# 2:4-sparse linear layer on one core: a first weight piece cut in two, a new hand-written order of the front, and unpacking DMAs in another order

## The chip, the core and the metric

One core of a Trainium2 chip. Five engines run their own instruction streams and meet at semaphores: TensorE (PE, matmuls; its weight loads are shown apart as PEld), VectorE (DVE), ScalarE (ACT), GpSimd (POOL) and SyncE (SP, which here issues DMAs). Sixteen DMA engines move the data. The metric is the device time of one execution in microseconds; smaller is better. Before the change it is 235.28 us, the median of 3 runs (235.22 to 235.59).

## The reference

```python
B, S, D = 16, 512, 1024            # x: (16, 512, 1024), w: (1024, 1024), b: (1024), all bf16
wg = w.reshape(D // 4, 4, D)       # groups of 4 along k
mag = jnp.abs(wg)
order = jnp.argsort(mag, 1)
thr = jnp.take_along_axis(mag, order[:, 2:3, :], 1)
mask = mag >= thr                  # the two largest of each four stay
wp = (wg * mask).reshape(D, D)
out = einsum("bsd,df->bsf", x, wp) + b
```

So the weight matrix is pruned 2:4 along k, and 8192 tokens are multiplied with it: 64 tiles of 128 tokens, each with k = 1024 and 1024 output columns.

## The kernel before

**Two stretches.** The main loop (lines 286 to 303) is plain: each tile of 128 tokens takes 16 matmuls of 512 columns (8 blocks of k by two halves of the output), DVE adds the bias out of PSUM, ACT issues the store. It needs x transposed (done by transposing DMAs, `issue_batch`) and the pruned weights in natural order of k, `wp_nat[h]` (h is the half of the output columns). Ahead of it stands the front, which has to load, prune and unpack the weights while PE already works on the first T = 10 tiles.

**How the weights come.** `w` is seen as `(g p m) f`: g is a half of k (512 rows), p the partition, m the place in a group of four. So a group's four values lie in one partition, and pruning is elementwise work on DVE. It goes by *pieces* `(g, c0, c1)`: half of k and a range of output columns. For each piece `abs_piece` (A) makes magnitudes, on DVE or on ACT, and `prep_piece` (P) runs seven DVE operations (lines 131 to 141): max and min of pairs, the threshold, the mask, the product back into `w_gh`.

**How PE uses them.** For the first half of k (g = 0), the token tiles are transposed on PE itself with an identity (`transpose_half`, T) in the order of (p, m), and copied out of PSUM by ACT (`copy_half`, C), so that the pruned weights can be used in the layout they have. For the second half (g = 1), x comes through one transposing DMA in natural order (`xg1`, line 96), and the weights must first be *unpacked*: `unpack` (U) issues, for each j of its range, one DMA from 32 partitions of `w_gh` into all 128 partitions of one k block of `wp_nat`. The first half of k is unpacked too, but only the main loop uses that.

**Tokens of FRONT.** The order of the whole front is written out by hand as a string of tokens (lines 229 to 239) and executed by the loop under it; everything is kept in program order, so each engine runs its part of the tokens strictly one after the other. `W` and `w` are warm-up matmuls on zeros of 512 and 128 columns. `M.i.t` is PE's four matmuls (m or j = 0 to 3) of piece i for tile t, tiles 0 to 7; a matmul is as wide as the piece. `X.q.t` does the same for tiles 8 and 9 over a whole half of the output, with q = 2g + h. `V.h.t` copies the finished g = 0 sum from PSUM to SBUF on ACT (`to_stage`), which frees the bank; `O.h.t` adds the g = 1 sum to it on DVE; `B.h.t` adds the bias on DVE and, with the second half, issues the store (those that stay over are done in the main loop). `U.g.h.c0.c1[.j0.j1]` are unpacking DMAs, `L.n` a transposing load of x for the main loop; both are issued from SP. PSUM has eight banks, given out in turn: a T or the first M of a new (q, tile) takes the next one, and has to wait for whoever reads the old contents out.

**Queues around the change.** SP issues, in this order: the loads of w and x, the bias, the transposing load of `xg1` (8.21 to 17.44 us), the unpacking DMAs in the order of the U tokens, and then the loads for the main loop. An SP instruction that waits (an unpacking DMA waits for the P that made its piece) holds all behind it. The first weight load, g = 0 and columns 0 to 256, is two DMAs on SP and ACT; columns 256 to 512 are one, columns 512 to 1024 one, and g = 1 two.

Lines touched by the diff: the list `pieces` (60), the string (230 to 238) and the rule which A runs on ACT (246).

Of the kernel before, what the change touches and what calls it, by code (L numbers as in the profile page):

```python
# [10 lines left out]
def kernel(  # L11
# [8 lines left out]
    P = 128  # L20
# [7 lines left out]
    B, S, D = x.shape  # L28
# [10 lines left out]
    T = 10  # L39
# [17 lines left out]


    wv = w.rearrange("(g p m) f -> p g m f", g=2, m=4)
    pieces = [(0, 0, 256), (0, 256, 512), (0, 512, 768), (0, 768, 1024), (1, 0, 256), (1, 256, 512), (1, 512, 1024)]  # L60
    w_gh = {(g, h): const.tile([P, 4, FH], bf16, name=f"w_{g}_{h}") for g in range(2) for h in range(2)}

    def w_of(i):
        g, c0, c1 = pieces[i]
        return w_gh[(g, c0 // FH)][:, :, c0 % FH:c0 % FH + c1 - c0]
# [39 lines left out]
    def warm(n):  # L105
        K(nc.tensor.matmul(bank[7][:, :n], lhsT=zeros[:, :P], rhs=zeros[:, :n], start=True, stop=True))  # L106
# [3 lines left out]
    def abs_piece(i, on_act):  # L110
        g, c0, c1 = pieces[i]
        n = c1 - c0
        if n <= 256:
            mag = mags_pool.tile([P, 4, n], bf16, name="mag")[:]
        else:
            mag = const.tile([P, 4, n], bf16, name=f"mag_{i}")[:]
        if on_act:
            K(nc.scalar.activation(mag, w_of(i), Act.Abs))  # L118
        else:
            K(nc.vector.tensor_single_scalar(  # L120
                mag.bitcast(u16), w_of(i).bitcast(u16), 0x7FFF, op=Alu.bitwise_and))
        mags[i] = mag

    def prep_piece(i):
        g, c0, c1 = pieces[i]
        n = c1 - c0
        mag = mags.pop(i)
        magv = mag.rearrange("p (a j) f -> p a j f", j=2)
        hi = tmp.tile([P, 2, FH], bf16, name="hi")[:, :, :n]
        lo = tmp.tile([P, 2, FH], bf16, name="lo")[:, :, :n]  # L130
        K(nc.vector.tensor_tensor(hi, magv[:, :, 0, :], magv[:, :, 1, :], op=Alu.max))  # L131
        K(nc.vector.tensor_tensor(lo, magv[:, :, 0, :], magv[:, :, 1, :], op=Alu.min))  # L132
        t1 = tmp.tile([P, FH], bf16, name="t1")[:, :n]
        t2 = tmp.tile([P, FH], bf16, name="t2")[:, :n]
        K(nc.vector.tensor_tensor(t1, hi[:, 0, :], hi[:, 1, :], op=Alu.min))
        K(nc.vector.tensor_tensor(t2, lo[:, 0, :], lo[:, 1, :], op=Alu.max))  # L136
        thr = tmp.tile([P, FH], bf16, name="thr")[:, :n]
        K(nc.vector.tensor_tensor(thr, t1, t2, op=Alu.max))
        mask = tmp.tile([P, 4, FH], bf16, name="mask")[:, :, :n]
        K(nc.vector.tensor_tensor(mask, mag, thr[:, None, :].to_broadcast([P, 4, n]), op=Alu.is_ge))  # L140
        K(nc.vector.tensor_tensor(w_of(i), w_of(i), mask, op=Alu.mult))  # L141
# [4 lines left out]
    def unpack(g, h, c0, c1, j0=0, j1=4):  # L146
        for j in range(j0, j1):
            K(nc.sync.dma_start(wp_nat[h][:, 4 * g + j, c0:c1], w_gh[(g, h)][32 * j:32 * (j + 1), :, c0:c1]))
# [4 lines left out]
    def transpose_half(t):  # L153
        own[(0, t)] = next_bank()
        xv = xh[t].rearrange("p (q m) -> p m q", m=4)
        dst = bank[own[(0, t)]][:].bitcast(bf16)[:, :4 * P].rearrange("p (m q) -> p m q", m=4)
        for m in range(4):
            K(nc.tensor.transpose(dst[:, m, :], xv[:, m, :], ident[:]))  # L158

    def copy_half(t):  # L160
        xt = const.tile([P, 4, P], bf16, name=f"xT_{t}")
        src = bank[own[(0, t)]][:].bitcast(bf16)[:, :4 * P].rearrange("p (m q) -> p m q", m=4)
        K(nc.scalar.copy(xt[:], src))  # L163
        xT[t] = xt


    def mm_part(q, t, c0, c1):
        g, h = divmod(q, 2)
        if c0 == 0 and q > 0:
            own[(q, t)] = next_bank()  # L170
        dst = bank[own[(q, t)]][:, c0:c1]
        for m in range(4):
            if g == 0:
                lhs, rhs = xT[t][:, m, :], w_gh[(0, h)][:, m, c0:c1]
            else:
                lhs, rhs = xg1[:, m, t * P:(t + 1) * P], wp_nat[h][:, 4 + m, c0:c1]
            K(nc.tensor.matmul(dst, lhsT=lhs, rhs=rhs, start=c0 == 0 and m == 0, stop=c1 == FH and m == 3))  # L177
# [11 lines left out]
    def to_stage(h, t):  # L189
        stage[(h, t)] = const.tile([P, FH], fp32, name=f"stage{h}_{t}")  # L190
        K(nc.scalar.copy(stage[(h, t)][:], bank[own[(h, t)]][:]))  # L191

    def add_stage(h, t):
        st = stage[(h, t)][:]
        K(nc.vector.tensor_tensor(st, bank[own[(2 + h, t)]][:], st, op=Alu.add))  # L195

    def add_bias(h, t):
        f = slice(h * FH, (h + 1) * FH)
        K(nc.vector.tensor_tensor(get_o(t)[:, f], stage.pop((h, t))[:], bias_sb[:, f], op=Alu.add))  # L199
        if (1 - h, t) not in stage:  # L200
            store(t)
# [10 lines left out]
    def issue_batch(t0, nb):  # L212
        if nb < 8:
            xt = const.tile([P, KT, nb * P], bf16, name=f"xTs{t0}")
        else:
            xt = xtb.tile([P, KT, nb * P], bf16, name="xTb")
        K(nc.sync.dma_start_transpose(out=xt[:], in_=xf[t0 * P:(t0 + nb) * P, :]))
        for j in range(nb):
            xN[t0 + j] = xt[:, :, j * P:(j + 1) * P]
# [7 lines left out]


    FRONT = """
        A.0 P.0 W W W W W W W W T.0 T.1 C.0 w w w T.2 T.3 C.1 C.2 w w w w w w w w M.0.0 C.3 T.4 T.5 A.1 C.4 M.0.1  # L230
        P.1 T.6 C.5 T.7 M.0.2 C.6 M.0.3 C.7 M.0.4 M.0.5 A.2 M.0.6 M.0.7 A.3 P.2 M.1.0 M.1.1 A.4 M.1.2 M.1.3 V.0.0
        M.1.4 V.0.1 M.1.5 P.3 M.1.6 V.0.2 M.1.7 V.0.3 T.8 T.9 M.2.0 C.8 M.2.1 C.9 X.0.8 V.0.4 P.4 U.0.0.0.512.0.2
        U.1.0.0.256 X.0.9 V.0.5 A.5 M.2.2 M.2.3 V.0.6 M.3.0 M.3.1 V.0.7 M.2.4 P.5 U.0.0.0.512.2.4 U.1.0.256.512
        V.0.8 M.2.5 M.3.2 V.0.9 M.2.6 A.6 M.2.7 M.3.3 M.3.4 M.3.5 V.1.0 P.6 U.0.1.0.512 U.1.1.0.512 L.0 L.1 L.2
        M.3.6 V.1.1 M.3.7 X.1.8 V.1.2 V.1.3 X.1.9 V.1.4 M.4.0 V.1.5 M.4.1 M.4.2 V.1.6 M.4.3 V.1.7 M.4.4 M.5.0 V.1.8
        M.4.5 O.0.0 V.1.9 M.4.6 M.5.1 B.0.0 M.4.7 O.0.1 M.5.2 M.5.3 B.0.1 M.5.4 O.0.2 M.5.5 M.5.6 O.0.3 M.5.7 O.0.4
        X.2.8 O.0.5 X.2.9 O.0.6 M.6.0 O.0.7 M.6.1 O.0.8 O.0.9 M.6.2 O.1.0 M.6.3 O.1.1 M.6.4 O.1.2 M.6.5 O.1.3 O.1.4
        M.6.6 O.1.5 M.6.7 O.1.6 X.3.8 O.1.7 X.3.9 O.1.8 O.1.9
    """
    for tok in FRONT.split():  # L240
        k, *n = tok.split(".")
        n = [int(c) for c in n]
        if k in "Ww":
            warm(FH if k == "W" else P)
        elif k == "A":
            abs_piece(n[0], n[0] >= 2)
        elif k == "P":
            prep_piece(n[0])
        elif k == "T":
            transpose_half(n[0])  # L250
        elif k == "C":
            copy_half(n[0])
        elif k == "M":
            g, c0, c1 = pieces[n[0]]
            h = c0 // FH
            mm_part(2 * g + h, n[1], c0 - h * FH, c1 - h * FH)
        elif k == "X":
            mm_part(n[0], n[1], 0, FH)
        elif k == "V":
            to_stage(*n)  # L260
        elif k == "O":
            add_stage(*n)
        elif k == "B":
            add_bias(*n)
        elif k == "U":
            unpack(*n)
        elif k == "L":
            issue_batch(*batches[n[0]])
# [63 lines left out]
```

## Time and profile before

| | us |
|---|---|
| Median of 3 runs | 235.28 (235.22 to 235.59) |
| Profiled execution | 235.46 |
| its span, first to last instruction | 233.7 |
| PE busy | 227.4 (97% of the span) |
| DVE busy | 117.2 (50%) |
| ACT busy | 22.3 (10%) |

The profile page gives, besides, the span in 40 slices of 5.8 us with the busy tenths of each engine:

```profile
PE   7999999999999999999999999999999999999994
...
DVE  4799799884856244244334334324424423433433
ACT  2899700000000000000000000000000000000000
...
PEclk9999999999999999999999999999999999999999
```

PE is busy from end to end but for the first and last slice. The front fills the first seven or eight slices, and there DVE (pruning) and ACT (copies) are nearly as busy as PE; then both go down. A busy PE is no proof that the work is useful: warm-up matmuls count as well. In a row of the timeline the first number is the start, the second the time from the first start to the last end of the merged instructions; matmuls are pipelined, so that the distance of two starts is smaller than a single duration (0.273 us for 256 columns, 0.379 for 512).

### The profile page before, as it was taken

The page shows a single profiled execution, that of the slowest core. Times are in us where ns is not written, and L with a number is a line of the kernel's source. Part 1 is how long each engine was busy: PE and PEld are TensorE (multiplying, and loading weights), DVE is VectorE, ACT ScalarE, POOL GpSimd, SP SyncE. Part 2 cuts the span into 40 slices and gives each one's busy share as a digit, 9 for nine tenths or more (in the row PEclk, how much of TensorE's full clock was granted, in tenths as well). Part 3 has the DMA queues.
Part 4 walks back from the last instruction along what each step waited for, and adds up shares of the span by engine and source line. Part 5 has one row for each costly group of instructions (what it writes and reads, how often), then busy time and mean ns, then how long its engine had stood idle before and what let it go on. Part 6 is the DMA issues. An engine that isn't in the chain of part 4 may idle for free.

```text
span 233.7 us, 2919 instructions
## 1 busy us (share of the span) xinstructions
PE 227.4 (97%) x1175; PEld 114.3 (49%) x1195; DVE 117.2 (50%) x202; ACT 22.3 (10%) x37; POOL 0.7 (0%) x6
## 2 busy tenths in 40 slices
PE   7999999999999999999999999999999999999994
PEld 2788774444444444444444444444444444444443
DVE  4799799884856244244334334324424423433433
ACT  2899700000000000000000000000000000000000
POOL 1000000000000000000000000000000000000000
PEclk9999999999999999999999999999999999999999
DMA  6998599999975212991239821695228942122122
GB/s 184 351 259 140 113 197 245 258 267 220 288 287 211 90 57 77 235 284 67 90 89 267 230 91 45 129 306 160 81 90 201 240 145 88 47 90 93 45 90 90
DMA packets 77404, 38.19 MB, mean 163 GB/s; under 512 B 62544, under 2 KB 69200, under 8 KB 77392
## 3 DMA queue, kind: packets, MB, share of 16 engines
q1 hardware_dynamic: 67504, 20.84, 43.8%
q10 hardware_dynamic: 9888, 17.17, 20.4%
q8 instruction: 9, 0.15, 0.2%
q14 instruction: 3, 0.02, 0.0%
HBM read 3.67 MB, written 16.78 MB: 88 GB/s over the span
## 4 chain that ended last, share of the span: by engine, by line
PE 94%; DMA 3%; issue 1%; SPq 1%; ACT 0%; DVE 0%
PE bank L296 78%; PE bank L177 14%; DMA xh<-in_x_dram 3%; PE bank L274 2%; SPq L69 0%; PE bank L158 0%; ACT xT L163 0%; SPq L77 0%; DVE o_sb L283 0%
## 5 line engine op out<-in xcount | busy, mean ns | idle before, releaser
L296 PE MATMUL bank<-wp_nat,xTb 128*128 128x512 bf16 x737 | 161.7, 379 | 0.8
L204 DVE TENSOR_TENSOR o_sb<-bank,bias_sb 128x512 bf16<-128x512 f32 x106 | 68.1, 686 | 101.2 <-PE bank L296 93.3
L296 PEld LDWEIGHTS <-xTb 128*128 128x128 bf16 x752 | 73.6, 98 | 88.7
L296 PE MATMUL bank<-wp_nat,xTs 128*128 128x512 bf16 x94 | 20.8, 379 | 0.1
L177 PE MATMUL bank<-w,xT 128*128 128x256 bf16 (+1 forms) x142 | 18.0, 283 | 0.1
L177 PE MATMUL bank<-wp_nat,xg 128*128 128x256 bf16 (+1 forms) x111 | 17.5, 318 | 0.1
L177 PEld LDWEIGHTS <-xT 128*128 128x128 bf16 x144 | 14.0, 98 | 3.1
L296 PEld LDWEIGHTS <-xTs 128*128 128x128 bf16 x96 | 9.4, 98 | 11.3
L199 DVE TENSOR_TENSOR o_sb<-stage,bias_sb 128x512 bf16<-128x512 f32 x20 | 12.7, 685 | 3.4 <-DMA out_dram<-o_sb 3.3
L195 DVE TENSOR_TENSOR stage<-bank,stage 128x512 f32<-128x512 f32 x20 | 12.8, 686 | 2.6 <-PE bank L177 2.3
L177 PEld LDWEIGHTS <-xg 128*128 128x128 bf16 x112 | 11.0, 98 | 6.4
L191 ACT COPY stage<-bank 128x512 f32<-128x512 f32 x20 | 10.3, 662 | 0.0
L118 ACT ACTIVATE mag<-w 128x1024 bf16<-128x1024 bf16 (+1 forms) x5 | 6.1, 1245 | 0.3 <-DVE t L136 0.3
L106 PE MATMUL bank<-zeros 128*128 128x128 bf16 (+1 forms) x19 | 4.5, 392 | 1.2 <-DVE zeros L99 1.2
L163 ACT COPY xT<-bank 128x512 bf16<-128x512 bf16 x10 | 5.3, 593 | 2.7 <-PE bank L158 2.7
L141 DVE TENSOR_TENSOR w<-w,mask 128x1024 bf16<-128x1024 bf16 (+1 forms) x7 | 5.4, 769 | 0.2
L140 DVE TENSOR_TENSOR mask<-mag,thr 128x1024 bf16<-128x1024 bf16 (+1 forms) x7 | 5.4, 768 | 0.2
L158 PE MATMUL bank<-ident,xh 128*128 128x128 bf16 x40 | 3.1, 221 | 0.9 <-DMA xh<-in_x_dram 0.9
L274 PE MATMUL bank<-wp_nat,xTb 128*128 128x128 bf16 (+2 forms) x32 | 3.7, 272 | 0.0
L158 PEld LDWEIGHTS <-xh 128*128 128x128 bf16 x40 | 2.5, 114 | 2.3 <-DMA xh<-in_x_dram 2.3
L131 DVE TENSOR_TENSOR hi<-mag 128x512 bf16<-128x512 bf16 (+1 forms) x7 | 3.2, 459 | 0.1
L132 DVE TENSOR_TENSOR lo<-mag 128x512 bf16<-128x512 bf16 (+1 forms) x7 | 3.2, 457 | 0.0
(16 smaller groups left out, 15.9 us busy)
## 6 DMA issues: line engine op xcount, KB each, us to landing
out_dram<-o_sb ACTq DMA_DIRECT2D x63, 256.0 KB, 2.1
w<-in_w_dram SPq DMA_DIRECT2D x3, 512.0 KB, 8.3
wp_nat<-w SPq DMA_DIRECT2D x12, 128.0 KB, 3.1
xh<-in_x_dram SPq DMA_DIRECT2D x3, 256.0 KB, 6.5
xh<-in_x_dram ACTq DMA_DIRECT2D x2, 256.0 KB, 5.1
wp_nat<-w SPq DMA_DIRECT2D x8, 64.0 KB, 2.1
w<-in_w_dram SPq DMA_DIRECT2D x1, 256.0 KB, 6.5
bias_sb<-in_b_dram SPq DMA_DIRECT2D x1, 256.0 KB, 7.7
```

The source lines that it names most:

```text
L118: K(nc.scalar.activation(mag, w_of(i), Act.Abs))
L140: K(nc.vector.tensor_tensor(mask, mag, thr[:, None, :].to_broadcast([P, 4, n]), op=Alu.is_ge))
L141: K(nc.vector.tensor_tensor(w_of(i), w_of(i), mask, op=Alu.mult))
L158: K(nc.tensor.transpose(dst[:, m, :], xv[:, m, :], ident[:]))
L163: K(nc.scalar.copy(xt[:], src))
L177: K(nc.tensor.matmul(dst, lhsT=lhs, rhs=rhs, start=c0 == 0 and m == 0, stop=c1 == FH and m == 3))
L191: K(nc.scalar.copy(stage[(h, t)][:], bank[own[(h, t)]][:]))
L195: K(nc.vector.tensor_tensor(st, bank[own[(2 + h, t)]][:], st, op=Alu.add))
L199: K(nc.vector.tensor_tensor(get_o(t)[:, f], stage.pop((h, t))[:], bias_sb[:, f], op=Alu.add))
L204: K(nc.vector.tensor_tensor(get_o(t)[:, h * FH:(h + 1) * FH], bank[bk][:], bias_sb[:, h * FH:(h + 1) * FH], op=Alu.add))
L274: K(nc.tensor.matmul(bank[bk][:, :c1 - c0], lhsT=xN[t][:, kt, :], rhs=wp_nat[h][:, kt, c0:c1], start=kt == 0, stop=kt == KT - 1))
L296: K(nc.tensor.matmul(bank[bks[h]][:], lhsT=xN[t][:, kt, :], rhs=wp_nat[h][:, kt, :], start=kt == 0, stop=kt == KT - 1))
```

## The change

1. The piece (g = 0, columns 0 to 256) becomes two pieces of 128 columns. There are eight pieces instead of seven, so the numbers in A, P and M of all later pieces go up by one. The loads stay as they are. Each of the two has its own magnitudes and seven DVE operations on half the elements; M.0 and M.1 are now 64 matmuls of 128 columns in place of 32 of 256.
2. Magnitudes: before, pieces 0 and 1 on DVE and the others on ACT; now pieces 0 and 2 (columns 0 to 128 and 256 to 512) on DVE and all others, the new piece 1 too, on ACT.
3. A new FRONT string. The eight `w` after T.2, T.3 and C.2 are gone, the three after C.0 stay. M tokens of the first two pieces stand between the transposes and go on in another mixture; T.8 and T.9 come after M.2.0 to M.2.3; M.3 and M.4 (columns 512 to 1024 of g = 0) are interleaved, and M.6.0 (g = 1, columns 256 to 512) comes after M.5.3, where its counterpart M.5.0 came after M.4.4. One more bias addition, B.0.2, is done in the front.
4. Unpacking: the two DMAs U.0.0.0.512.0.2, first half of k, j = 0 and 1, came first of all and now come after the four of U.1.0.0.256. The four of U.0.1.0.512, which came ahead of U.1.1.0.512, are split: two ahead, two behind. The number and sizes of the DMAs are the same, 20.

```diff
-    pieces = [(0, 0, 256), (0, 256, 512), (0, 512, 768), (0, 768, 1024), (1, 0, 256), (1, 256, 512), (1, 512, 1024)]
+    pieces = [(0, 0, 128), (0, 128, 256), (0, 256, 512), (0, 512, 768), (0, 768, 1024),
+              (1, 0, 256), (1, 256, 512), (1, 512, 1024)]
...
-        A.0 P.0 W W W W W W W W T.0 T.1 C.0 w w w T.2 T.3 C.1 C.2 w w w w w w w w M.0.0 C.3 T.4 T.5 A.1 C.4 M.0.1
-        P.1 T.6 C.5 T.7 M.0.2 C.6 M.0.3 C.7 M.0.4 M.0.5 A.2 M.0.6 M.0.7 A.3 P.2 M.1.0 M.1.1 A.4 M.1.2 M.1.3 V.0.0
-        M.1.4 V.0.1 M.1.5 P.3 M.1.6 V.0.2 M.1.7 V.0.3 T.8 T.9 M.2.0 C.8 M.2.1 C.9 X.0.8 V.0.4 P.4 U.0.0.0.512.0.2
-        U.1.0.0.256 X.0.9 V.0.5 A.5 M.2.2 M.2.3 V.0.6 M.3.0 M.3.1 V.0.7 M.2.4 P.5 U.0.0.0.512.2.4 U.1.0.256.512
-        V.0.8 M.2.5 M.3.2 V.0.9 M.2.6 A.6 M.2.7 M.3.3 M.3.4 M.3.5 V.1.0 P.6 U.0.1.0.512 U.1.1.0.512 L.0 L.1 L.2
-        M.3.6 V.1.1 M.3.7 X.1.8 V.1.2 V.1.3 X.1.9 V.1.4 M.4.0 V.1.5 M.4.1 M.4.2 V.1.6 M.4.3 V.1.7 M.4.4 M.5.0 V.1.8
...
+        A.0 A.1 P.0 W W W W W W W W T.0 T.1 C.0 w w w T.2 P.1 T.3 C.1 M.0.0 C.2 M.0.1 C.3 M.0.2 T.4 T.5 A.2 C.4
+        M.0.3 M.1.0 P.2 M.1.1 C.5 M.0.4 T.6 T.7 C.6 M.0.5 M.1.2 C.7 M.0.6 M.1.3 A.3 M.1.4 M.0.7 M.1.5 M.1.6 M.1.7
+        A.4 P.3 M.2.0 M.2.1 V.0.0 M.2.2 M.2.3 V.0.1 T.8 M.2.4 C.8 T.9 M.2.5 P.4 C.9 M.2.6 A.5 M.2.7 X.0.8 V.0.2
+        X.0.9 V.0.3 V.0.4 M.3.0 P.5 U.1.0.0.256 U.0.0.0.512.0.2 M.3.1 V.0.5 M.3.2 V.0.6 M.3.3 M.4.0 V.0.7 M.3.4 A.6
+        M.3.5 M.4.1 V.0.8 P.6 U.1.0.256.512 U.0.0.0.512.2.4 U.0.1.0.512.0.2 M.4.2 M.4.3 V.0.9 M.3.6 A.7 M.3.7 M.4.4
+        M.4.5 M.4.6 V.1.0 P.7 U.1.1.0.512 U.0.1.0.512.2.4 L.0 L.1 L.2 M.4.7 V.1.1 X.1.8 V.1.2 X.1.9 V.1.3 M.5.0
+        V.1.4 M.5.1 V.1.5 M.5.2 V.1.6 M.5.3 M.6.0 V.1.7 M.5.4 V.1.8 O.0.0 M.5.5 M.6.1 V.1.9 B.0.0 M.5.6 O.0.1 M.5.7
...
+        O.0.9 M.7.2 O.1.0 M.7.3 O.1.1 M.7.4 O.1.2 O.1.3 M.7.5 O.1.4 M.7.6 O.1.5 M.7.7 O.1.6 X.3.8 B.0.2 O.1.7 X.3.9
...
-            abs_piece(n[0], n[0] >= 2)
+            abs_piece(n[0], n[0] not in (0, 2))
```

More of the change, by code (lines that the diff above doesn't have):

```diff
@@ L229 @@
     FRONT = """
-        A.0 P.0 W W W W W W W W T.0 T.1 C.0 w w w T.2 T.3 C.1 C.2 w w w w w w w w M.0.0 C.3 T.4 T.5 A.1 C.4 M.0.1
-        P.1 T.6 C.5 T.7 M.0.2 C.6 M.0.3 C.7 M.0.4 M.0.5 A.2 M.0.6 M.0.7 A.3 P.2 M.1.0 M.1.1 A.4 M.1.2 M.1.3 V.0.0
-        M.1.4 V.0.1 M.1.5 P.3 M.1.6 V.0.2 M.1.7 V.0.3 T.8 T.9 M.2.0 C.8 M.2.1 C.9 X.0.8 V.0.4 P.4 U.0.0.0.512.0.2
-        U.1.0.0.256 X.0.9 V.0.5 A.5 M.2.2 M.2.3 V.0.6 M.3.0 M.3.1 V.0.7 M.2.4 P.5 U.0.0.0.512.2.4 U.1.0.256.512
-        V.0.8 M.2.5 M.3.2 V.0.9 M.2.6 A.6 M.2.7 M.3.3 M.3.4 M.3.5 V.1.0 P.6 U.0.1.0.512 U.1.1.0.512 L.0 L.1 L.2
-        M.3.6 V.1.1 M.3.7 X.1.8 V.1.2 V.1.3 X.1.9 V.1.4 M.4.0 V.1.5 M.4.1 M.4.2 V.1.6 M.4.3 V.1.7 M.4.4 M.5.0 V.1.8
-        M.4.5 O.0.0 V.1.9 M.4.6 M.5.1 B.0.0 M.4.7 O.0.1 M.5.2 M.5.3 B.0.1 M.5.4 O.0.2 M.5.5 M.5.6 O.0.3 M.5.7 O.0.4
-        X.2.8 O.0.5 X.2.9 O.0.6 M.6.0 O.0.7 M.6.1 O.0.8 O.0.9 M.6.2 O.1.0 M.6.3 O.1.1 M.6.4 O.1.2 M.6.5 O.1.3 O.1.4
-        M.6.6 O.1.5 M.6.7 O.1.6 X.3.8 O.1.7 X.3.9 O.1.8 O.1.9
+        A.0 A.1 P.0 W W W W W W W W T.0 T.1 C.0 w w w T.2 P.1 T.3 C.1 M.0.0 C.2 M.0.1 C.3 M.0.2 T.4 T.5 A.2 C.4
[5 more added lines that the diff above has]
+        V.1.4 M.5.1 V.1.5 M.5.2 V.1.6 M.5.3 M.6.0 V.1.7 M.5.4 V.1.8 O.0.0 M.5.5 M.6.1 V.1.9 B.0.0 M.5.6 O.0.1 M.5.7
+        M.6.2 B.0.1 M.6.3 M.6.4 O.0.2 M.6.5 O.0.3 M.6.6 M.6.7 O.0.4 X.2.8 O.0.5 X.2.9 O.0.6 M.7.0 O.0.7 O.0.8 M.7.1
+        O.0.9 M.7.2 O.1.0 M.7.3 O.1.1 M.7.4 O.1.2 O.1.3 M.7.5 O.1.4 M.7.6 O.1.5 M.7.7 O.1.6 X.3.8 B.0.2 O.1.7 X.3.9
+        O.1.8 O.1.9
     """
```

## The prediction

> **What bounds the kernel now.** I read the page's chain of waits first, then the TensorE (PE) row of the timeline over the first 45 us, then VectorE (DVE), the SP queue and the DMA view of the same stretch.
>
> ```profile
> PE 94%; DMA 3%; issue 1%; SPq 1%; ACT 0%; DVE 0%
> ...
> q8 instruction: 9, 0.15, 0.2%
> ```
>
> The end is set by PE. From 43.85 us on matmuls of 512 columns follow each other every 0.216 us, and the diff touches none of them: the question is when that stretch begins. Timeline, PE (start, duration, what, count, idle time before):
>
> ```profile
> 5.24 0.64 PE L158 MATMUL bank<-ident,xh 128*128 128x128 bf16 x8 [0.46 <-DMA xh<-in_x_dram]
> 5.71 0.33 PE L106 MATMUL bank<-zeros 128*128 128x128 bf16 x3
> 5.88 0.61 PE L158 MATMUL bank<-ident,xh 128*128 128x128 bf16 x8
> 6.33 0.61 PE L106 MATMUL bank<-zeros 128*128 128x128 bf16 x8
> 6.92 0.60 PE L177 MATMUL bank<-w,xT 128*128 128x256 bf16 x4
> 7.67 0.64 PE L158 MATMUL bank<-ident,xh 128*128 128x128 bf16 x8 [0.15 <-DMA xh<-in_x_dram]
> 9.00 0.64 PE L158 MATMUL bank<-ident,xh 128*128 128x128 bf16 x8 [0.26 <-DMA xh<-in_x_dram]
> 9.48 2.78 PE L177 MATMUL bank<-w,xT 128*128 128x256 bf16 x24
> 26.48 2.35 PE L177 MATMUL bank<-wp_nat,xg 128*128 128x256 bf16 x20
> ```
>
> Steps follow from these. A matmul of 256 columns comes every 0.109 us ((2.78 - 0.27) / 23), one of 128 every 0.056 us ((0.61 - 0.22) / 7). The x24 are the first 256-column piece for tiles 2 to 7; they end, and the second piece begins, at 9.48 + 24 x 0.109 = 12.10. From 9.00 on PE has no pause that matters. Timeline, DVE:
>
> ```profile
> 8.23 0.43 DVE L120 TENSOR_SCALAR mag<-w 128x1024 uint16<-128x1024 uint16 x1 [1.36 <-DMA w<-in_w_dram]
> 10.95 0.69 DVE L141 TENSOR_TENSOR w<-w,mask 128x1024 bf16<-128x1024 bf16 x1
> 19.53 0.69 DVE L141 TENSOR_TENSOR w<-w,mask 128x1024 bf16<-128x1024 bf16 x1
> ```
>
> Columns 256:512 of the first half of k start when their load lands (8.21) and are pruned at 10.95 + 0.69 = 11.64, a little ahead of PE. Columns 0:256 of the second half are done at 20.22. Timeline, SP queue, and the DMA view of single issues:
>
> ```profile
> 20.25 3.78 SPq L148 DMA_DIRECT2D wp_nat<-w  x6
> 24.13 3.93 SPq L148 DMA_DIRECT2D wp_nat<-w  x5
> 26.68 1.38 SPq L148 DMA_DIRECT2D wp_nat<-w  x1
> 28.11 4.53 SPq L148 DMA_DIRECT2D wp_nat<-w  x7
> ```
>
> An unpacking DMA holds SP for 0.60 us, the next starts 0.645 us after it; the one at 26.68 took 1.38. In the window 26.4 to 26.5 the DMA view has
>
> ```profile
> q8 instruction: 1, 0.02, 76.4%
> ```
>
> that is 0.764 x 0.1 us x 16 engines = 1.22 us on one DMA engine, begun at 26.45: one of the nine 16 KB blocks of instructions. The SP issue that met it ended 1.61 us after its start; the other such meeting (block at 17.70, issue 18.23 of 1.05 us) ended 1.58 us after. So an issue that begins up to 0.645 us behind a block is held until about 1.6 us behind it: 0.35 to 1.0 us late, 0.68 on average.
>
> **The change, part by part.** (1) Eight small warm-up matmuls go: 8 x 0.056 = 0.45 us of PE. They stand in front of work that waits for DVE and DMA, so the gain is what (4) leaves. On the clock: the eight large warm-ups follow each other every 0.43 us, later matmuls of that width every 0.216, while the clock row reads 9 throughout; after 5.24 all run at the faster step. The longest pause that I get for the new order is under 0.5 us, so I take no loss; bound above, if the faster step were lost for the 64 small matmuls, 64 x 0.056 = 3.6 us, less the slack. The Trainium skill (TensorE: Matmul & The Clock Gate, Part 1) says PE falls back to half clock after an idle window of some 3.4 us, which speaks against taking fillers away; by it nothing is lost at pauses this short.
>
> (2) Halving. DVE rows give 0.28, 0.42, 0.69 us for 256, 512, 1024 elements, about 0.155 + 0.00052 per element, so 0.22 for 128 (estimate). The first half takes about 2.25 us from 3.46 (0.32, 0.20, 0.20, 0.14, 0.26, 0.26, 0.45, 0.42 from start to start), to 5.7 instead of 6.86; the second, whose magnitudes ACT makes in about 0.60 us from 3.80, takes 1.9, to 7.6. That is before 8.21, so the next piece still starts on its load and ends at 11.64. On PE, 64 x 0.056 in place of 32 x 0.109 is 0.09 us more, beside the wait of (4).
>
> (3) PE's new head (new numbers of pieces from here on). T.0, T.1, three fillers, T.2, T.3 to 6.33; the copies xT.0, .1, .2 end at 6.28, 6.77, 7.25 as before, each freeing 4 x 0.056 = 0.22 us of M.0; T.4, T.5 at 7.67 (their load); M.0.3, M.1.0, M.1.1 to 8.81, M.0.4 to 9.03, T.6, T.7 to 9.50, M.0.5, M.1.2 to 9.95; M.0.6 waits for its copy until 10.1; then six units of 0.22 and M.1.7's end at 11.65 to 11.7.
>
> (4) M.2.0 needs the prune that ends at 11.64; 0.05 more from DVE's end to PE's start (first piece before: 6.86 to 6.92): 11.70. The same work stood done at 12.10. **Gain 0.40 us**, and no more, since a load fixes 11.64. M.2 to M.4, T.8, T.9 and four X follow without a stop: PSUM copies on ACT run ahead (V.0.2, which frees M.3.0's bank, at 15.96 + 0.6; M.3.0 starts at 17.3). A.6 ends at 19.9 by ACT's steps of 0.48 and 0.95, its piece starts at 20.14; if that cover went, the unpacking would be late by as much. M.5.0 comes at 26.48 - 0.40 = 26.08.
>
> (5) Unpacking. SP now waits from 17.5 until 20.25 and issues four DMAs (second half of k, 0:256), two of the first half, and at 24.13 four for 256:512. That is the old timetable from 20.25 on; only the two that went ahead at 17.56 moved back. What PE wants has moved: M.6.0, the first user of 256:512, stood (under the old number M.5.0) five units behind old M.4.0, at 28.66, and now stands four behind new M.5.0, 26.08 + 4 x 0.436 = 27.82, its fourth matmul at 28.15. Undisturbed, the fourth DMA (issued 26.04) lands 2.1 us later, 28.15: no slack. Before, with the block at 26.45 between, it landed 2.9 us after issue, at 28.98, just ahead of its use at 29.02.
>
> And the block moves. At 26.45 PE had done 203 matmuls, 406 instructions; by 49.41, the next block, about 681. The new order has 24 more matmuls in front, so instruction 406 stands 24 matmuls before M.5.0 (8 wide, 16 of 256 columns: 3.47 us), at 22.6; within some 20 instructions, 22 to 23.7. There SP is issuing, and everything behind slips by 0.35 to 1.0 us. Taking the mean, 0.68: landing 28.83, fourth matmul 28.86, **a stall of 0.70 us**; at the ends 0.38 and 1.03. A block on 24.1 to 26 itself gives 0.8, as before at 28.98. What stands behind in PE's queue, M.5.4 to the end, all waits. The Trainium skill (Runtime: NRT & Kernel Launch, Instruction fetch mechanics) says that blocks of 256 instructions are fetched while the engine runs on, mostly hidden. By that sentence the stall is nil and the time 0.40 us shorter; in the row PE was indeed not held, but SP was.
>
> (6) Later: the second half's columns 512:1024 are unpacked behind 14 DMAs, as before; the last landed at 32.02 + 3.7 = 35.7, its user began at 35.87. With (5) PE is there no sooner. Two DMAs now stand behind them, so the transposing loads start 1.3 us later (34.0 for 32.68), land about 39 and are wanted at 43.9: covered by 4 us. B.0.2 (0.60 us of DVE) lies beside PE.
>
> Sum: -0.40 + 0.70 = **+0.30 us**; the profiled execution goes from 235.46 (span 233.7 and 1.76 around it) to 235.76, and the median, 0.18 below it, from 235.28 to **235.6**. With the ends of (5), -0.02 to +0.63: 235.3 to 235.9.
>
> **Rivals.** *No hold on SP* (20%): the block falls where SP isn't issuing, or is absorbed; the 0.40 stays, 234.9. For: PE itself never waited for a block. Against: both blocks that met an unpacking issue lengthened it. *Slower by a late load* (15%): the first block (17.70 before, with 272 PE instructions done) comes early, near 10 us, and holds one engine for 1.2 us under columns 512:1024 of w, which landed at 10.46, just as ACT wanted them. DVE's pieces from 11.57 on and all unpacking then slip 1.1 us, the stall is 1.1 to 2.1, the time 236.0 to 237.0, about 236.3; it decides once that load is over 0.5 us late. Against: at the same instruction count the block falls at about 14.5, behind the loads. *The fillers were the loss* (5%): the eight (0.45) and the pauses around the loads (0.15, 0.26) all come back, 234.4. Against: PE would run into 11.64.
>
> **Numbers.** The forecast has 60%. Runs of this kernel spread over 0.37 us, so I call 0.2% (0.47 us) the limit of what is told from no change. A third of the forecast lies above +0.47 (stall over 0.87), two thirds within. Slower: 0.21 + 0.15 = 0.36. Faster: the filler case 0.05, and a third of the 20%, 0.06: 0.11. Same: 0.53. Range 234.7 to 236.2: it takes in the unheld case and the nearer part of the late load.
>
> **What would show it.** M.2.0 at 11.7; 256-column units on the second half of k from 26.1; an instruction block at 22 to 24 and an SP issue over 0.9 us behind it; a PE pause of 0.4 to 1.0 us at 27.9 to 28.9 waiting for an unpacking DMA; the 512-wide stretch of the main loop at 44.1. No such pause, with that stretch at 43.45, is the first rival; a DVE pause at 11.6 the second.

## The result, and the profile after

| | before | changed |
|---|---|---|
| median | 235.20 (234.88 to 235.59, 8 runs) | 236.06 (235.71 to 236.92, 8 runs) |
| profiled execution | 235.46, span 233.7 | 236.07, span 234.3 |
| changed to before | | 1.0041, 95% interval 1.0025 to 1.0058 |

The changed kernel is 0.86 us slower in the median, 0.61 us in the two profiled executions; the profiled execution of before lies 0.26 above its median, that of the changed kernel at its median. Beside other executions of before, in two later comparisons, the ratio came out at 1.0023 (1.0011 to 1.0036) and 1.0008 (0.9994 to 1.0021). So it is slower by 0.2 to 0.4% in two comparisons, and not clearly slower in the third.

The page's chain of waits, by engine, in the changed kernel:

```profile
PE 86%; DVE 7%; DMA 4%; SPq 1%; issue 1%
```

Before it read PE 94%: the chain ran along PE from 9 us on. Now it leaves PE in the front and goes back through a DMA and SP to DVE's pruning and a load of w. The timeline of PE over the first 12 us (start, duration, what, count, idle time before):

```profile
4.74 1.04 PE L159 MATMUL bank<-ident,xh 128*128 128x128 bf16 x8
5.57 0.40 PE L107 MATMUL bank<-zeros 128*128 128x128 bf16 x3
5.81 0.61 PE L159 MATMUL bank<-ident,xh 128*128 128x128 bf16 x8
6.26 1.15 PE L178 MATMUL bank<-w,xT 128*128 128x128 bf16 x12
7.74 0.64 PE L159 MATMUL bank<-ident,xh 128*128 128x128 bf16 x8 [0.34 <-DMA xh<-in_x_dram]
8.22 1.06 PE L178 MATMUL bank<-w,xT 128*128 128x128 bf16 x16
9.11 0.64 PE L159 MATMUL bank<-ident,xh 128*128 128x128 bf16 x8
9.59 2.68 PE L178 MATMUL bank<-w,xT 128*128 128x128 bf16 x39
```

The first matmuls on weights begin at 6.26 instead of 6.92, in units of four small matmuls with waits between: the first twelve start over 1.15 - 0.22 = 0.93 us, where 11 x 0.056 would be 0.62. To add up: M.0 and M.1 are 12 + 16 + 36 matmuls; the last three of the x39 (the row is cut off by the window's end) are already wider ones, of M.2.0, which starts at 11.78. The pruning of its weights, on DVE:

```profile
8.32 0.43 DVE L121 TENSOR_SCALAR mag<-w 128x1024 uint16<-128x1024 uint16 x1 [0.56 <-DMA w<-in_w_dram]
11.03 0.69 DVE L142 TENSOR_TENSOR w<-w,mask 128x1024 bf16<-128x1024 bf16 x1
```

The load landed at 8.30 (8.21 before), the prune ended at 11.73, and PE followed 0.05 later; its own last matmul of M.1.7 had begun at 11.72, so that it was free at just that moment too. So far the gain is there: PE is at work on the second half of k at 26.16, before at 26.48. Then, PE from there on:

```profile
26.16 2.13 PE L178 MATMUL bank<-wp_nat,xg 128*128 128x256 bf16 x18
28.55 0.27 PE L178 MATMUL bank<-wp_nat,xg 128*128 128x256 bf16 x1 [0.27 <-DMA wp_nat<-w]
29.19 0.60 PE L178 MATMUL bank<-wp_nat,xg 128*128 128x256 bf16 x4 [0.36 <-DMA wp_nat<-w]
44.46 1.89 PE L298 MATMUL bank<-wp_nat,xTs 128*128 128x512 bf16 x8
```

Sixteen matmuls of M.5 and two of M.6.0, then two stops. Undisturbed the starts are 0.109 apart: the 18th started at 28.01, the next at 28.55, the one behind it at 29.19, so the stops cost 0.43 and 0.53 us. (The idle column shows less, because it counts from the modelled end of a pipelined matmul.) The main loop begins at 44.46 instead of 43.85. What the third and fourth matmul of M.6.0 waited for, in SP's queue:

```profile
20.42 3.21 SPq L149 DMA_DIRECT2D wp_nat<-w  x5
...
23.67 1.37 SPq L149 DMA_DIRECT2D wp_nat<-w  x1
...
25.14 2.49 SPq L149 DMA_DIRECT2D wp_nat<-w  x4
```

and in the DMA view of the window 23.4 to 23.5:

```profile
q8 instruction: 1, 0.02, 73.6%
```

A 16 KB block of instructions took one DMA engine from 23.46 for 0.736 x 0.1 x 16 = 1.18 us; the SP issue that began behind it took 1.37 us instead of 0.60, and the four DMAs that M.6.0 needs went out from 25.14 to 27.63. The last of them, issued at 27.02, landed 2.1 us later, at 29.15, and the page's chain runs over it (start, duration):

```profile
27.02 2.12 DMA wp_nat<-w
29.19 5.29 PE bank L178 x46
```

### The profile page after: what moved, and what is told of

It is laid out like the page before. It is cut to its first block, busy times and chain, and to the rows that moved or that the text cites. A ratio compares the mean times of both kernels' runs of the same rounds, so it can differ in the third digit from the quotient of the medians.

```text
span 234.3 us, 2977 instructions
## 1 busy us (share of the span) xinstructions
PE 227.8 (97%) x1199; PEld 114.9 (49%) x1219; DVE 117.9 (50%) x209; ACT 22.8 (10%) x38; POOL 0.7 (0%) x6
## 4 chain that ended last, share of the span: by engine, by line
PE 86%; DVE 7%; DMA 4%; SPq 1%; issue 1%
PE bank L298 78%; PE bank L178 7%; DMA w<-in_w_dram 3%; DVE mask L141 1%; PE bank L276 1%; DVE w L142 1%; DVE hi L132 1%; DVE lo L133 1%; DMA wp_nat<-w 1%; DVE thr L139 1%; DVE t L137 1%; DVE t L136 1%; SPq L149 1%; SPq L78 0%; SPq L70 0%
## 5 line engine op out<-in xcount | busy, mean ns | idle before, releaser
L178 PE MATMUL bank<-w,xT 128*128 128x256 bf16 (+2 forms) x174 | 18.6, 262 | 0.2
L178 PEld LDWEIGHTS <-xT 128*128 128x128 bf16 x176 | 14.5, 98 | 3.2 <-ACT xT L164 0.4
L119 ACT ACTIVATE mag<-w 128x1024 bf16<-128x1024 bf16 (+2 forms) x6 | 6.8, 1149 | 0.0
L141 DVE TENSOR_TENSOR mask<-mag,thr 128x1024 bf16<-128x1024 bf16 (+2 forms) x8 | 5.5, 692 | 0.3
L142 DVE TENSOR_TENSOR w<-w,mask 128x1024 bf16<-128x1024 bf16 (+2 forms) x8 | 5.5, 692 | 0.3
L107 PE MATMUL bank<-zeros 128*128 128x512 bf16 (+1 forms) x11 | 4.0, 527 | 1.2 <-DVE zeros L100 1.2
L159 PE MATMUL bank<-ident,xh 128*128 128x128 bf16 x40 | 3.7, 239 | 0.3 <-DMA xh<-in_x_dram 0.3
L132 DVE TENSOR_TENSOR hi<-mag 128x512 bf16<-128x512 bf16 (+2 forms) x8 | 3.4, 421 | 0.1
L133 DVE TENSOR_TENSOR lo<-mag 128x512 bf16<-128x512 bf16 (+2 forms) x8 | 3.3, 418 | 0.0
```

## The experiments

In all of them, "the pause" is the time that PE loses in M.6.0 against an even step of 0.109 us. Each is compared with 35 runs of before on its own chip; experiments on the same chip (e1 to e4, e5 to e8, e9 to e12) share these runs, so that they aren't independent of each other. The ratios are those on record; they can differ a little from the quotient of the two medians.

**Is it the order of unpacking?** The changed kernel with the old order of the U tokens:

```diff
-P.5 U.1.0.0.256 U.0.0.0.512.0.2 ... P.6 U.1.0.256.512 U.0.0.0.512.2.4 U.0.1.0.512.0.2 ... P.7 U.1.1.0.512 U.0.1.0.512.2.4
+P.4 U.0.0.0.512.0.2 ... P.5 U.1.0.0.256 ... P.6 U.0.0.0.512.2.4 U.1.0.256.512 ... P.7 U.0.1.0.512 U.1.1.0.512
```

> The changed kernel with only the unpacking order put back to the old one. Theory (an instruction block holds the SP queue, and M.6.0 now stands too early for what lands): from 20.4 us on SP issues the same number of DMAs before the four of 256:512, so their last landing stays near 29.1, PE pauses 0.8 to 1.0 us in M.6.0, and the kernel is 0.5 to 1.0 us slower than before, like the changed one. Rival (the order of unpacking is what costs): the pause goes, 0.2 to 0.4 us faster than before.

Measured: 235.58 us against 235.23, ratio 1.0011 (0.9998 to 1.0025). The block came at 23.22, one SP issue took 1.26 us, the last of the four landed at 28.79, the pause was 0.65 us; PE behind it:

```profile
28.83 1.36 PE L178 MATMUL bank<-wp_nat,xg 128*128 128x256 bf16 x11 [0.35 <-DMA wp_nat<-w]
```

So the pause stays, a bit smaller than said, and the time lies between the two expectations, nearer to the theory. Going back to the old order of unpacking doesn't take the pause away: in both orders two other DMAs stand ahead of the four of 256:512.

**Is it the place of 256:512 in SP's queue?** The four DMAs of 256:512 directly behind the four of 0:256:

```diff
-P.5 U.1.0.0.256 U.0.0.0.512.0.2 ... P.6 U.1.0.256.512 U.0.0.0.512.2.4 U.0.1.0.512.0.2
+P.5 U.1.0.0.256 ... P.6 U.1.0.256.512 U.0.0.0.512.0.2 U.0.0.0.512.2.4 U.0.1.0.512.0.2
```

> The changed kernel with the four unpacking DMAs of the second half of k, columns 256:512, directly behind the four of 0:256; the two of the first half that stood between follow them. Theory: even with one SP issue held by 0.8 us they start at 23.3 and the last lands near 27.9, before M.6.0's fourth matmul at 28.2; no pause, the 0.3 us won at the head stay: 0.2 to 0.4 us faster than before. Rival (the landing is late for want of DMA bandwidth, not for the place in the queue): landing still near 29, pause still over 0.5 us, not faster than before.

Measured: 234.85 us, ratio 0.9986 (0.9974 to 0.9998). With a block at 22.54 one issue took 1.25 us here as well, but the last of the four landed at 27.49, and PE didn't stop:

```profile
25.75 4.42 PE L178 MATMUL bank<-wp_nat,xg 128*128 128x256 bf16 x39
43.10 1.24 PE L298 MATMUL bank<-wp_nat,xTs 128*128 128x512 bf16 x5
```

39 matmuls in (4.42 - 0.27) / 38 = 0.109 us each: no pause. As the theory said.

**Is it the place of M.6.0 in PE's order?** SP as in the changed kernel, PE takes all of M.5 first:

```diff
-M.5.3 M.6.0 V.1.7 M.5.4 V.1.8 O.0.0 M.5.5 M.6.1 V.1.9 B.0.0 M.5.6 O.0.1 M.5.7 M.6.2
+M.5.3 V.1.7 M.5.4 V.1.8 M.5.5 V.1.9 M.5.6 M.5.7 M.6.0 O.0.0 M.6.1 B.0.0 O.0.1 M.6.2
```

> The changed kernel with SP's order untouched, but PE takes all eight M.5 before M.6.0. Theory: M.6.0 starts at 29.65, after the landing at 29.15; no pause, 0.2 to 0.4 us faster than before. Rival (the lost time sits elsewhere, in the head or in DVE's late start of O.0.0): slower than before by 0.3 or more, or a new PE pause at X.2.8 or in the M.7 units, which wait for DVE to free banks.

Measured: 234.92 us, ratio 0.9980 (0.9970 to 0.9990). SP and PE:

```profile
23.27 1.46 SPq L149 DMA_DIRECT2D wp_nat<-w  x1
...
25.84 4.42 PE L178 MATMUL bank<-wp_nat,xg 128*128 128x256 bf16 x39
43.19 1.03 PE L298 MATMUL bank<-wp_nat,xTs 128*128 128x512 bf16 x4
```

SP was held even longer (1.46 us), the last of the four landed at 28.86, and it cost nothing, since M.6.0 comes at 29.3. The late O.0.0 made no new wait: PE ran through to the main loop.

**Is it the instruction block?** More instructions for PE, and nothing else: pieces 2 and 3 as two matmuls of 128 columns each.

```diff
-            mm_part(2 * g + h, n[1], c0 - h * FH, c1 - h * FH)
+            cuts = [c0, c0 + P, c1] if n[0] in (2, 3) else [c0, c1]
+            for a, z in zip(cuts, cuts[1:]):
+                mm_part(2 * g + h, n[1], a - h * FH, z - h * FH)
```

> The changed kernel with the matmuls of pieces 2 and 3 (256 columns) each issued as two of 128 columns on PE: 64 matmuls more, no other engine's work changed. Theory: the second instruction block, which comes by PE's instruction count, moves from 23.5 to 16 to 18 us, out of the stretch in which SP unpacks; no SP issue over 0.7 us between 20.4 and 28, the last of 256:512 lands near 28.4, M.6.0's fourth matmul stands near 28.4 as well; pause under 0.2. The small matmuls cost 0.1 to 0.2 us. Sum: 0 to 0.2 us faster than before, 0.6 to 0.9 faster than the changed kernel. Rival (the long SP issue has nothing to do with PE's instructions): it stays at 23.7, and the kernel is 0.1 to 0.2 us slower than the changed one, 0.8 to 1.1 slower than before.

Measured: 234.95 us, ratio 0.9990 (0.9976 to 1.0004). The second block moved to 19.68 (16 to 18 was expected), the third to 31.03, and SP:

```profile
19.96 5.14 SPq L149 DMA_DIRECT2D wp_nat<-w  x8
...
24.49 2.55 SPq L149 DMA_DIRECT2D wp_nat<-w  x4
...
25.95 4.31 PE L178 MATMUL bank<-wp_nat,xg 128*128 128x256 bf16 x38
```

Eight issues in 5.14 us, 0.64 each, none held; the last of 256:512 landed at 27.94, no pause. At the third block an SP issue at 31.0 took 1.38 us, where nobody waits for it. Nothing but PE's instructions was changed, the block moved, and the long issue and the pause went with it. Two things temper this. The count of instructions isn't the whole rule for the block: in the other thirteen profiles 201 to 210 matmuls stand in the trace ahead of the second block, here 229. And luck had a part: the block did not leave SP's stretch, as expected, but met the first unpacking issue, and that one took its usual 0.61 us (last section). With e1 to e3 the cause of the pause is shown all the same: the four DMAs of 256:512 go out behind a long SP issue, and M.6.0 stands too early for them.

**The changed kernel again,** on the chip of the next three:

> The changed kernel itself once more, on the chip and beside the same runs of before as the next three. Theory: an instruction block near 23.3, one SP issue of 1.2 to 1.4 us, the last of 256:512 landing at 28.7 to 29.2, PE paused 0.6 to 1.0 us in M.6.0; 0.3 to 0.9 us slower than before. Against e1 (old unpacking order): the same within 0.3 us if the order of unpacking costs nothing; if it costs, this one stays 0.5 or more above e1.

Measured: 235.60 us against 235.07, ratio 1.0023 (1.0011 to 1.0036). Block at 22.84, an SP issue of 1.49 us, landing at 28.66, a pause of 0.97 us. Its median is that of e1 (235.58), on another chip.

**Were the eight fillers a loss?** e3 with them put back behind T.3:

```diff
-T.2 P.1 T.3 C.1 M.0.0
+T.2 P.1 T.3 C.1 w w w w w w w w M.0.0
```

> e3 (no pause in M.6.0) with the eight small warm-up matmuls put back behind T.3. Theory: they run where PE otherwise waits for the loads of x (pauses of 0.25 and 0.5 us before 7.8), so M.2.0 starts within 0.1 us of where it does in e3; the same time as e3 within 0.15 us, 0.2 to 0.4 us faster than before. Rival (the fillers were the loss): 0.45 us slower than e3.

Measured: 235.01 us, ratio 0.9991 (0.9976 to 1.0005), against 234.97 for e8 beside it. The 0.45 us of fillers don't show in the times. M.2.0 came at 11.94, 0.48 later than in e3, which was not expected, but the load of x that T.4 needs landed later by the same 0.48 (7.89 for 7.41), and PE still waits for it behind the fillers:

```profile
6.14 0.61 PE L107 MATMUL bank<-zeros 128*128 128x128 bf16 x8
6.59 0.93 PE L178 MATMUL bank<-w,xT 128*128 128x128 bf16 x12
7.93 0.64 PE L159 MATMUL bank<-ident,xh 128*128 128x128 bf16 x8 [0.41 <-DMA xh<-in_x_dram]
```

Against before the run isn't clearly faster, which had been expected of it.

**Does the halved piece do it?** e3 with columns 0:256 pruned in one go, PE's order and its small matmuls left:

```diff
+    def prep_range(i):
+        return (0, 0, 256) if i == 0 else pieces[i]
...
-        A.0 A.1 P.0 ... T.2 P.1 T.3
+        A.0 P.0 ... T.2 T.3
```

> e3 with columns 0:256 pruned as one piece again (one magnitude operation on DVE and seven DVE operations, as before the change), PE's matmuls and their order as in e3. Theory: M.0.0 starts at 6.9 instead of 6.3, the three units M.0.0 to M.0.2 still stand before T.4, which waits for its load until 7.6 or so, and M.2.0 still starts when the next piece is pruned: the same time as e3 within 0.15 us; then halving brings nothing by itself and the order is all. Rival (the halved piece is what lets PE catch up): M.2.0 0.2 to 0.6 us later and the kernel slower than e3 by as much.

Measured: 235.03 us, ratio 0.9993 (0.9985 to 1.0001), level with e6 and e8. But M.2.0 didn't start where its prune ended: PE began M.0.0 at 7.11 and had M.1.7 done at 11.75, while that prune ended at 11.19. T.4, whose x had landed at 7.26, began at 7.78, behind the M.0 that waited for the whole prune. So halving could have been worth up to 0.5 us in that execution (an estimate); in the times no difference shows.

**Both remedies together:** e3 with the U order of e2.

> e2 and e3 together: the unpacking of 256:512 directly behind 0:256, and M.6.0 behind the eight M.5. Theory: neither has a pause left to remove, so together they bring no more than each alone: 0.2 to 0.5 us faster than before, within 0.15 us of e3. Rival: there is still a wait behind M.6.0 that only the earlier landing takes away; then 0.2 us or more faster than e3.

Measured: 234.97 us, ratio 0.9991 (0.9981 to 1.0001). No pause, and no more than each alone; the gain over before is smaller than said.

**Halving alone,** in the kernel before:

```diff
-    pieces = [(0, 0, 256), (0, 256, 512), ...
+    pieces = [(0, 0, 128), (0, 128, 256), (0, 256, 512), ...
-        A.0 P.0 ... M.0.0 ... M.0.1
+        A.0 A.1 P.0 P.1 ... M.0.0 M.1.0 ... M.0.1 M.1.1
```

> The kernel before with the first weight piece halved and nothing else (its order and unpacking as before, M.0.t and M.1.t in a row, ACT making the magnitudes of piece 1). Theory (the gain at the head comes from the order, halving only allows M.0 to begin earlier): PE starts the third piece at 12.1 to 12.3, as before; 32 more matmuls bring the second instruction block forward to about 23, SP's issues slip by 0.8 us, the last of 256:512 lands at 28.9 to 29.2, where M.6.0's fourth matmul stands at 29.1: at most 0.15 us of pause. Sum 0 to 0.3 us slower than before. Rival (halving is the gain): 0.3 us or more faster than before.

Measured: 235.34 us against 235.31, ratio 1.0000 (0.9989 to 1.0010). No gain, as the theory had it. The third piece starts at 12.05, the block comes at 22.60, and the issue beside it takes 1.49 us. The profiled execution (236.00, the slowest of its twelve) has a pause of 0.60 us, more than expected: SP began the four of 0:256 at 20.60 instead of 20.25, and the last of 256:512 landed at 29.50. So halving alone already moves the block from 26.45 to 22.60, into SP's unpacking.

**The old unpacking order without the pause:** e3 with the U tokens of before.

> e3 with the old order of unpacking. Theory (unpacking the second half of k ahead brings nothing, since SP has nothing else to do before 20 us): the same as e3 within 0.15 us. Rival: the two DMAs in front make the four of 0:256 late, 0.3 us or more slower than e3.

Measured: 234.68 us against 235.31, ratio 0.9979 (0.9966 to 0.9993); e11 beside it 234.84. So unpacking the second half of k first brings nothing: the two DMAs that went out at 17.86 and 18.52 were gone before the prune of 0:256 let SP go on at 19.77.

**e3 again, beside the changed kernel:**

> e3 once more, beside the changed kernel on the same chip. Theory: no pause in M.6.0; 0.2 to 0.5 us faster than before and 0.5 to 0.9 us faster than the changed kernel.

Measured: 234.84 us, ratio 0.9981 (0.9968 to 0.9993). No pause.

> The changed kernel beside the other three. Theory: PE paused 0.6 to 1.0 us in M.6.0, 0.3 to 0.9 us slower than before.

Measured: 235.44 us, ratio 1.0008 (0.9994 to 1.0021), with a pause of 1.09 us in the profiled execution (235.87):

```profile
28.28 0.27 PE L178 MATMUL bank<-wp_nat,xg 128*128 128x256 bf16 x1 [0.37 <-DMA wp_nat<-w]
28.94 1.25 PE L178 MATMUL bank<-wp_nat,xg 128*128 128x256 bf16 x10 [0.39 <-DMA wp_nat<-w]
```

The changed kernel is 0.60 us behind e11; against before it isn't clearly slower on this chip.

**What the times are made of.** All fourteen profiles (before, changed, e1 to e12) add up in the same way: from the start of M.2.0 to that of M.5.0 (M.1.0 and M.4.0 by the old numbers) 14.38 us, in e4 with its extra matmuls 14.54; from there to the main loop 17.34 or 17.35 plus the pause; from there to the end 189.82 to 189.84. So only two things differ from kernel to kernel, the start of M.2.0 and the pause, and the pause costs its whole length. M.2.0 starts at 12.10 before and at 12.05 in e9; with the new order of PE it starts between 11.24 and 11.94.

So the change with M.6.0 put behind M.5.7 (e3, e11, or e10) is faster than before, by ratios of 0.9979 to 0.9981 on two chips, whose intervals don't reach 1 (0.31 to 0.63 us in the medians), and 0.60 us faster than the changed kernel beside it (e11, e12). On the third chip it ran only in altered form (e6, e7, e8): 0.9991 to 0.9993, with intervals that reach 1.

## Why the prediction was right, and where it was off

The direction of the sum and its main mechanism were right: a gain at the head, a block of instructions that moves onto SP's unpacking, and a pause in M.6.0 that takes back more than the gain. The size was too small: +0.30 us were forecast and counted as no change; the profiles show +0.61, the medians +0.86, +0.53 and +0.13. The 236.06 lies inside the range, but above the 235.9 that the bounds of the pause allow. The medians of the first comparison lie further apart than the profiles because the profiled execution of before, from which the sum started, was 0.26 slower than its kernel's median. No change had 53% and slower, by more than 0.47 us, 36%: in two of three comparisons it was the latter. Step 4's reason for the size of the gain was wrong.

- *Step 4, the gain of 0.40.* Measured 0.32 (26.48 to 26.16); the load that the step counts on landed 0.09 later. But the step says "no more, since a load fixes 11.64", and that held in no other profile. In the changed kernel's profile the prune and PE were ready together. In the eleven other profiles with the new order the load landed between 7.29 and 8.42, the prune was done 0.08 to 0.60 us before M.2.0 started, and M.2.0 came one even step (0.056) behind PE's own last small matmul, 3.98 to 4.01 us behind T.4. In e8:

```profile
10.28 0.69 DVE L142 TENSOR_TENSOR w<-w,mask 128x1024 bf16<-128x1024 bf16 x1
9.38 2.68 PE L178 MATMUL bank<-w,xT 128*128 128x128 bf16 x39
```

Pruned at 10.97, M.2.0 at 11.57, in the same even row of 2.68 us as in the changed kernel. So step 3's row, PE behind the loads and copies of x, sets the gain. That the forecast number came close rests on the two having been equal (11.70, and 11.65 to 11.7) in the timetable that it used.

- *Step 5, the pause of 0.70.* Measured 0.96. This is the term that was mis-sized, within its own bounds of 0.38 to 1.03. The last DMA landed at 29.15 instead of 28.83: SP was let go at 20.42 instead of 20.25 (the prune of 0:256 ended at 20.39, 0.17 later, as DVE's piece 512:768 had to wait for ACT's magnitudes, which were done at 11.71 instead of 11.54), the hold was 0.77 instead of the mean of 0.68, and 0.06 is spread over the other issues. PE itself was 0.08 later than forecast, which takes a little off. In three further profiles of the changed kernel or e1 the pause was 0.65, 0.97 and 1.09, the last above the bound. The step reads the 28.98 of before as "just ahead of its use at 29.02"; PE's even step would have brought that use at 28.98, and the matmul came 0.03 late, so that there was no slack before either.
- *The sum.* -0.32 + 0.96 = +0.64, against +0.61 measured at the start of the main loop; the 0.03 between them is the wait of before just named. Nothing else of size came in.
- *The place of the block.* Forecast 22.6, 22 to 23.7 allowed; it came at 23.46, and between 22.5 and 23.5 in the other kernels with this order of PE.
- *Step 1, fillers at no cost:* e6 agrees. *Step 2, halving only as a means:* e9 and e7 agree in the times; e7's profile shows that the whole prune can hold PE up at its start. *Step 6, everything later is covered:* the last of 512:1024 landed at 34.86 and no wait followed.
- *Rivals.* "No hold on SP" fell: in thirteen of fourteen profiles an issue beside the second block was held. The fourteenth is e4, where the rival's case came about, and there the gain stayed, 0.28 us in the medians for the 0.40 forecast. "A late load" fell: the first block came at 16.4, behind all loads of w. "The fillers were the loss" fell with e6.

The Trainium skill (Runtime: NRT & Kernel Launch, Instruction fetch mechanics) calls the cost of crossing a block of instructions mostly hidden. For PE that agrees with every trace here: no PE wait stands at a block. For SP's issues it doesn't: but for one in e4, an unpacking issue beside a block took 0.3 to 1.0 us longer, and through it PE paused 0.60 to 1.09 us in the changed kernel, e1 and e9, where M.6.0 comes early and two other DMAs go out ahead of the four that it needs.

## What to carry to other kernels

An order worked out from measured arrivals is good only as long as the arrivals stay: this one moved work forward by 0.3 us against a queue that had no slack, and whose timetable moves when the number of PE's instructions does. Before fitting an order tightly, look up which arrival had no slack before (here a landing at 28.98 that PE already waited 0.03 us for), and leave there more than the largest hold that the trace has shown (0.78 us before; later runs had 0.99). And test the parts alone: the fillers, halving and the order of unpacking, old against new, don't show in the times, the order of PE does, and moving M.6.0 and M.6.1 a few places back turned the loss into a gain.

## What the runs showed of the hardware that I had not expected

An unpacking issue that begins beside an instruction block is not late by chance. Fifteen that began between 0.04 us before the block and 0.52 behind its start all ended 0.29 to 0.41 us after the block did; eleven that began 0.14 to 0.57 us before it took their usual 0.54 to 0.62. Block start and duration from the DMA packets, the held issue from SP's queue, us, in five of them:

| run | block | block's end | held issue | its end | behind the block |
|---|---|---|---|---|---|
| before | 26.45 + 1.22 | 27.67 | 26.68 + 1.38 | 28.06 | 0.39 |
| changed | 23.46 + 1.18 | 24.64 | 23.67 + 1.37 | 25.04 | 0.40 |
| e3 | 23.02 + 1.31 | 24.33 | 23.27 + 1.46 | 24.73 | 0.40 |
| e4, third block | 31.03 + 0.96 | 31.99 | 31.00 + 1.38 | 32.38 | 0.39 |
| e10 | 22.74 + 0.93 | 23.67 | 22.94 + 1.11 | 24.04 | 0.37 |

A DMA that is on its way when the block comes lands late as well: in the changed kernel the one issued at 22.38 landed 3.4 us later, the three of its size before it 2.1 to 2.2. Why an issue waits for the block isn't shown. One case stands against a plain rule: in e4, with the block from 19.68 to 20.61, the issue at 19.96 took its usual 0.61 us. It was the first unpacking DMA of that run, with none under way before it; whether that is the reason was not tried.

The clock step of PE moves from run to run: in the changed kernel's profile the first eight transposes, at 4.74, still followed each other every 0.107 us, the later ones every 0.056. There it cost nothing, since T.4 had to wait for its load (landed 7.70, T.4 at 7.74). In e8 the slow step lasted until 6.6 us, and T.4 began 2.92 us behind T.0; in e1 and e10, with the fast step throughout, it was 2.30. So part of e8's late M.2.0 comes from there; step 1 and step 3 of the prediction took the fast step for the whole head.
